# A capped-attention and swish feed-forward kernel: output sums kept in DRAM instead of SBUF

## The chip, the cores and the metric

The kernel runs on one core of a Trainium2 chip, as one program. The metric is the device time of one execution in microseconds (us); the number given for a kernel is the median of its timed runs. The traces come from one profiled execution each; their clock starts at the first instruction.

## What is computed

```python
scores = cap * tanh(q @ k.T / sqrt(64) / cap)       # 4 batches, 12 heads, 448 tokens
attn = exp(scores - max) / (sum + 1e-09)
x = heads side by side of (attn @ v)                # 1792 tokens x 768
h = x @ w_in                                        # 768 x 2048
out = (h * sigmoid(h)) @ w_out                      # 1792 tokens x 768, float32
```

The attention comes first and leaves x in SBUF; the feed-forward part (called moe in the code) follows on the same core.

## The kernel before, in words

The weights arrive as 64-bit floats and are turned into 32-bit ones on the core (`decode`, whose steps alternate between ACT and DVE). To keep precision, each operand of the moe's matmuls is split into a high part and a small remainder, and every product is made of three matmuls: high by high, remainder by high, high by remainder.

The moe works through 16 slices of 128 hidden features (NF = 16), taken two at a time: 8 passes, `fp` = 0 to 7. The 1792 tokens are cut into four blocks, three of 512 tokens and one of 256. Two kinds of unit fill a pass:

- `h_unit` (L585): 18 matmuls that make the hidden values of one slice for one block in a PSUM bank. `gate` (L603) follows it: ACT's sigmoid, DVE's product, ACT's copy of the high part and, one slot later, DVE's subtraction for the remainder. Eight such units make a pass.
- `o_unit` (L629): 12 matmuls that multiply 128 gated tokens by the two slices' rows of w_out. The result, 128 tokens by 768, lies in one of three PSUM tiles `s`, in two halves of 384 columns (NO2). `add` (L655) takes it out of PSUM. Fourteen such units make a pass, one for each group of 128 tokens.

The order is written out by hand in `moe` (L673): o_units come in pairs, and one or two h_units lie between pairs. Inside a slot, what belongs to earlier slots is issued first (L711 to L717), then the slot's own gate or add. Each engine works through its own queue strictly in the order of issue. Under `manual_schedule` (L726) this order is kept as it is written.

In `add`, the sums of all passes live in SBUF: 14 tiles `acc` of 128 x 768, six in one pool and eight in a second pool, `acc2`, which is opened at L422 when the attention's last buffers are free. For each half, DVE copies the PSUM tile into `acc` in the first pass (L665) and adds it in the other seven (L667). In the last pass SyncE's queue (SP) stores the finished rows to `out` (L671): one transfer of 384 KB for each unit, and for the very last unit, named LAST, two of 192 KB, one for each half. LAST also makes its halves one after the other (L637), the second in a PSUM bank of its own.

GpSimd (POOL) issues loads of q, k, v and the first weights during the attention (L295, L299, L292, L552 to L556); after that it issues nothing. SP issues the remaining weight loads of the moe (L552 to L556).

At the end stands a fallback (L733 to L735). Every engine loads a flag (TENSOR_LOAD, L733) and branches on it (COMPARE_BRANCH, L734) past a general version of the kernel, `tile_general`, which does not run here. A hint for that branch is set for SP and DVE alone (L724). Behind the branch come each engine's closing waits and drains; the trace puts these on line 794, where the kernel's outermost block ends.

Of the kernel before, what the change touches and what calls it, by code (L numbers as in the profile page):

```python
# [9 lines left out]
F32 = mybir.dt.float32  # L10
# [3 lines left out]
AF = mybir.ActivationFunctionType  # L14
ALU = mybir.AluOpType
# [170 lines left out]
def tile_softcap_attention_swish_moe(  # L186
# [12 lines left out]
    nc = tc.nc  # L199
# [4 lines left out]
    NT, DM = out.shape  # L204
# [7 lines left out]
    NO2 = DM // 2  # L212
# [6 lines left out]
    core = ctx.enter_context(ExitStack())  # L219
# [13 lines left out]
    pool = lambda st, name, bufs, **kw: st.enter_context(tc.tile_pool(name=name, bufs=bufs, reuse_waits="tile", **kw))  # L233
# [106 lines left out]
    def flat(t):  # L340
        return t.rearrange("p a s -> p (a s)")
# [67 lines left out]
    def norm2(s, parts=(0, 1)):  # L409
        b, u = s // NU, s % NU  # L410
        cs = slice(b * S, (b + 1) * S)
        x = U[s]
        if 0 in parts:
            nc.vector.tensor_tensor(flat(x), flat(x), flat(RB.pop(s)), ALU.mult)
        if 1 not in parts:
            return
        xh, xl = XH[:, 2 * u:2 * u + 2, cs], XL[:, 2 * u:2 * u + 2, cs]
        nc.vector.tensor_copy(xh, x)
        nc.vector.tensor_tensor(xl, x, xh.bitcast(F32), ALU.subtract)
        if s == NS - 1:  # L420
            tail.close()
            MPOOL["acc2"] = pool(core, "acc2", 1, side="right")  # L422


    BACK = {
# [19 lines left out]
    def attention():  # L445
# [17 lines left out]
        for s in range(NS):  # L463
# [33 lines left out]
            if s + 1 == NS:  # L497
                norm2(s - 2)
# [8 lines left out]
            for t in (i, k):  # L507
                for n in range(2):
                    exp(t, n)
                    sums(t, n)  # L510
                if 1 < s < NS - 1:
                    norm2(s - 2, (t - i,))
                for j in range(KC):
                    pv(t, j)
# [4 lines left out]
        pv_rem(s)  # L519
        u_vals(s)  # L520
        norm2(s - 1)
        pv_sum(s)
        u_sums(s)
# [13 lines left out]
    NFP = NF // G  # L537
    NTT = NT // 128
    MPOOL = {}
# [109 lines left out]
                        )  # L649
        return pa  # L650

    ACC = {}
    LAST = (NFP - 1, NB - 1, (NT - blocks[-1][0]) // 128 - 1)

    def add(fp, blk, t, pa):  # L655
        tt = blocks[blk][0] // 128 + t
        if tt not in ACC:
            ACC[tt] = MPOOL["acc" if tt < 6 else "acc2"].tile([128, DM], F32, name=f"acc{tt}")
        a = ACC[tt]
        last = (fp, blk, t) == LAST  # L660
        for e in range(2):
            c0, c1 = e * NO2, (e + 1) * NO2
            ae = a[:, c0:c1]
            if fp == 0:
                nc.vector.tensor_copy(ae, pa[e][:, 0:NO2])  # L665
            else:
                nc.vector.tensor_tensor(ae, pa[e][:, 0:NO2], ae, ALU.add)  # L667
            if fp == NFP - 1 and (last or e == 1):
                c0 = c0 if last else 0
                row = slice(128 * tt, 128 * tt + 128)  # L670
                nc.sync.dma_start(out=out[row, c0:c1], in_=a[:, c0:c1])  # L671

    def moe():  # L673

# [31 lines left out]
        for n, (bg, c) in enumerate(seq):  # L706
            if c[0] == "h":
                ps = h_unit(*c[1:])
            else:
                ps = o_unit(*c[1:])  # L710
            back(n, 0)  # L711
            late = list(LATE)
            LATE.clear()
            for x in late:
                gate(*x)
            for m, steps in bg:
                decode(m, steps)  # L717
            if c[0] == "h":
                gate(*c[1:], ps)
            else:  # L720
                add(*c[1:], ps)
            back(n, 1)
            if n == len(seq) - 3:
                tc.mark_branch_hint_location("short", 0, engines=[mybir.EngineType.SP, mybir.EngineType.DVE])  # L724
# [74 lines left out]
```

## Time and profile before

| what | value |
|---|---|
| median of 3 timed runs | 632.49 us |
| lowest and highest of them | 632.38 and 633.51 us |
| span of the profiled execution | 629.8 us |
| TensorE (PE) busy in the span | 621.0 us, 99% |
| DVE busy | 423.7 us, 67% |
| ACT busy | 271.0 us, 43% |
| POOL busy | 39.7 us, 6% |
| granted TensorE clock, mean | 1.000 |

The span runs from the first to the last instruction that the profile shows. For the profiled execution the span is the only time there is; the timed median lies 2.7 us above it (632.49 - 629.8), which is what an execution has around its instructions. PE, DVE, ACT and POOL are engines, PEld is TensorE's weight load, SP is SyncE. A letter q behind an engine's name (POOLq, SPq) marks instructions of its sequencer, such as waits, branches and DMA issues, which don't count as busy time. Where a row says "to landing", it gives the time from the issue of a DMA until its data and its semaphore had arrived.

### The profile page before, as it was taken

The numbers are of one execution on the slowest core, as the hardware profiler recorded it, in microseconds if no ns is written. First come the engines' busy times: TensorE is split into PE (matmuls) and PEld (weight loads), VectorE is DVE, ScalarE is ACT, GpSimd is POOL, SyncE is SP. The second block draws the span as 40 slices with busy tenths as digits, with TensorE's granted clock in tenths as the row PEclk, the third lists the DMA queues.
The fourth block names the chain that finished last, engine by engine and source line by source line (L and its number), as shares of the span: only waits on it lengthen the run. The fifth ranks groups of instructions, "written<-read, shape, count | busy, mean of one in ns | idle before, by whom it ended". The sixth has DMA issues, their size and how long they took to land.

```text
span 629.8 us, 9243 instructions
## 1 busy us (share of the span) xinstructions
PE 621.0 (99%) x3750; PEld 483.8 (77%) x3750; DVE 423.7 (67%) x661; ACT 271.0 (43%) x333; POOL 39.7 (6%) x75
## 2 busy tenths in 40 slices
PE   7999999999999999999999999999999999999996
PEld 3333333334699989999998999899989989999996
DVE  1578889889775685755684677558656856674343
ACT  7999999999213222322322322222223323222110
POOL 2231331320000000000000000000000000000000
PEclk9999999999999999999999999999999999999999
DMA  6674766461220421212130222212121302100224
GB/s 198 181 223 133 224 184 170 134 223 43 48 51 1 150 52 51 50 51 51 50 101 1 60 67 75 50 51 52 50 52 51 100 1 51 50 1 2 100 101 154
DMA packets 21507, 54.16 MB, mean 86 GB/s; under 512 B 4753, under 2 KB 13457, under 8 KB 21457
## 3 DMA queue, kind: packets, MB, share of 16 engines
q1 hardware_dynamic: 16928, 33.53, 19.5%
q0 software_dynamic: 4528, 19.96, 10.1%
q8 instruction: 31, 0.51, 0.3%
q14 instruction: 20, 0.16, 0.1%
HBM read 42.47 MB, written 5.51 MB: 76 GB/s over the span
## 4 chain that ended last, share of the span: by engine, by line
PE 97%; ACT 1%; DMA 1%; SPq 0%; issue 0%; DVE 0%
PE s L643 37%; PE h L592 36%; PE o L363 9%; PE s L308 8%; PE s L380 3%; PE o L370 1%; PE s L320 1%; DMA QK<-in_qkv_dram 1%; PE s L592 1%; ACT P L338 1%; ACT P L330 0%; PE h L643 0%; ACT P L334 0%; SPq L295 0%; DVE acc L667 0%
## 5 line engine op out<-in xcount | busy, mean ns | idle before, releaser
L592 PE MATMUL h<-XH,w 128*128 128x512 f32 (+1 forms) x756 | 217.5, 363 | 0.0
L643 PE MATMUL s<-w,gh 128*128 128x384 f32 x892 | 191.3, 335 | 0.0
L643 PEld LDWEIGHTS s<-w,gh 128*128 128x128 f32 x892 | 157.9, 188 | 2.9
L592 PEld LDWEIGHTS h<-XH,w 128*128 128x128 f32 x756 | 136.7, 188 | 22.1 <-DVE U L387 0.7
L592 PE MATMUL h<-XL,w 128*128 128x512 f32 (+1 forms) x378 | 137.5, 364 | 0.0
L607 ACT ACTIVATE gf<-h 128x512 f32<-128x512 f32 (+1 forms) x63 | 34.2, 543 | 206.3 <-PE h L592 205.9
L643 PE MATMUL s<-w,gl 128*128 128x384 f32 x446 | 113.7, 335 | 0.0
L608 DVE TENSOR_TENSOR gf<-h,gf 128x512 f32<-128x512 f32 (+1 forms) x63 | 39.3, 623 | 106.6 <-ACT gf L607 106.5
L667 DVE TENSOR_TENSOR acc<-s,acc 128x384 f32<-128x384 f32 x195 | 99.2, 550 | 8.6 <-PE s L643 8.5
L643 PEld LDWEIGHTS s<-w,gl 128*128 128x128 f32 x446 | 80.9, 188 | 0.0
L592 PEld LDWEIGHTS h<-XL,w 128*128 128x128 f32 x378 | 71.2, 188 | 10.4
L338 ACT ACTIVATE P<-P,capt 128x896 f32<-128x896 f32 (+1 forms) x60 | 75.0, 1328 | 0.0
L330 ACT ACTIVATE P<-s,sct 128x896 f32<-128x896 f32 x72 | 65.8, 1004 | 3.8 <-DVE over L265 3.6
L618 DVE TENSOR_TENSOR gl<-gf,gh 128x512 fp32r<-128x512 f32 (+1 forms) x64 | 40.1, 626 | 38.9 <-ACT gh L614 38.9
L614 ACT ACTIVATE gh<-gf 128x512 fp32r<-128x512 f32 (+1 forms) x64 | 37.1, 579 | 59.3 <-DVE gf L608 59.3
L308 PE MATMUL s<-QK 64*64 64x448 f32 x576 | 59.5, 542 | 1.0 <-DMA QK<-in_qkv_dram 1.0
L363 PE MATMUL o<-P,VT 128*64 128x448 f32 x288 | 58.1, 547 | 1.8 <-ACT P L338 1.7
L363 PEld LDWEIGHTS o<-P,VT 128*64 128x64 f32 x288 | 18.6, 136 | 40.5 <-issue 22.2
L308 PEld LDWEIGHTS s<-QK 64*64 64x64 f32 x576 | 20.7, 133 | 36.8 <-ACT P L330 15.7
L575 ACT ACTIVATE w<-RAW 128x768 fp32r<-128x768 f32 x28 | 23.7, 845 | 57.0 <-DVE RAW L180 50.4
L169 ACT ACTIVATE KRV<-RAW 128x768 f32<-128x768 f32 x28 | 25.0, 893 | 16.5 <-DVE RAW L180 11.6
L577 DVE TENSOR_TENSOR w<-RAW,w 128x768 fp32r<-128x768 f32 x32 | 30.5, 953 | 1.3 <-ACT w L575 1.2
(65 smaller groups left out, 366.8 us busy)
## 6 DMA issues: line engine op xcount, KB each, us to landing
QK<-in_qkv_dram POOLq DMA_DIRECT2D x21, 480.0 KB, 4.1
RAW<-in_moe_w_out_dram SPq DMA_DIRECT2D x13, 768.0 KB, 4.4
R<-RT SPq DMA_DIRECT2D x96, 56.0 KB, 2.7
RAW<-in_moe_w_in_dram SPq DMA_DIRECT2D x13, 384.0 KB, 4.2
RAW<-in_moe_w_in_dram SPq DMA_DIRECT2D x26, 192.0 KB, 4.7
out_dram<-acc SPq DMA_DIRECT2D x13, 384.0 KB, 2.3
VT<-in_qkv_dram POOLq DMA_DIRECT2D x22, 192.0 KB, 5.1
RAW<-in_moe_w_out_dram POOLq DMA_DIRECT2D x3, 768.0 KB, 8.1
```

What stands on the lines that cost most here:

```text
L308: nc.tensor.matmul(ps[half(c), e, 0:S], q[half(e), k0:k0 + 64], q[half(e), 0:S], start=True, stop=True)
L330: nc.scalar.activation(out=p, in_=SP.pop((i, j))[:, :, 0:S], func=AF.Tanh, scale=sct[:, 0:1])
L338: nc.scalar.activation(out=p, in_=p, func=AF.Exp, scale=capt[:, 0:1])
L363: nc.tensor.matmul(O[s][half(e), e ^ t, 0:S], v, p, start=(j == 0), stop=False)
L577: nc.vector.tensor_tensor(WS[m][:, 1], f, WS[m][:, 0].bitcast(F32), ALU.subtract)
L592: nc.tensor.matmul(ps[:, 0:n], w[:, a, kk * 128:(kk + 1) * 128], x[:, kk, t0:t0 + n], start=(kk == 0 and a == 0 and x is XH), stop=(kk == ...
L607: nc.scalar.activation(out=gf[:, 0:n], in_=ps[:, 0:n], func=AF.Sigmoid)
L608: nc.vector.tensor_tensor(gf[:, 0:n], ps[:, 0:n], gf[:, 0:n], ALU.mult)
L614: nc.scalar.activation(out=gh[:, 0:n], in_=gf[:, 0:n], func=AF.Copy)
L618: nc.vector.tensor_tensor(gl[:, 0:n], gf[:, 0:n], gh[:, 0:n].bitcast(F32), ALU.subtract)
L643: nc.tensor.matmul(pa[e][:, 0:NO2], g[a][:, ts], w[:, b, e * NO2:(e + 1) * NO2], start=(z == 0 and a == 0 and b == 0), stop=(z == G - 1 an ...
L667: nc.vector.tensor_tensor(ae, pa[e][:, 0:NO2], ae, ALU.add)
```

## The change

The sums move from SBUF to DRAM. `add` no longer keeps a tile for each group of tokens; each unit is copied out of PSUM into one of four rotating staging tiles `st`, the first half by ACT and the second by DVE. Then GpSimd's queue sends the staging tile to the output's rows: as a plain store in the first pass, and as an accumulating DMA, which adds to what lies there, in the seven others. Each unit sends one transfer of 384 KB; LAST sends two of 192 KB. SP no longer stores anything. The second pool `acc2` goes.

```diff
-            MPOOL["acc2"] = pool(core, "acc2", 1, side="right")
...
-    ACC = {}
...
         tt = blocks[blk][0] // 128 + t
-        if tt not in ACC:
-            ACC[tt] = MPOOL["acc" if tt < 6 else "acc2"].tile([128, DM], F32, name=f"acc{tt}")
-        a = ACC[tt]
+        a = MPOOL["acc"].tile([128, DM], F32, tag="st", name="st", bufs=4)
         last = (fp, blk, t) == LAST
+        row = slice(128 * tt, 128 * tt + 128)
         for e in range(2):
             c0, c1 = e * NO2, (e + 1) * NO2
-            ae = a[:, c0:c1]
-            if fp == 0:
-                nc.vector.tensor_copy(ae, pa[e][:, 0:NO2])
+            if e == 0:
+                nc.scalar.activation(out=a[:, c0:c1], in_=pa[e][:, 0:NO2], func=AF.Copy)
             else:
-                nc.vector.tensor_tensor(ae, pa[e][:, 0:NO2], ae, ALU.add)
-            if fp == NFP - 1 and (last or e == 1):
+                nc.vector.tensor_copy(a[:, c0:c1], pa[e][:, 0:NO2])
+            if last or e == 1:
                 c0 = c0 if last else 0
-                row = slice(128 * tt, 128 * tt + 128)
-                nc.sync.dma_start(out=out[row, c0:c1], in_=a[:, c0:c1])
+                if fp == 0:
+                    nc.gpsimd.dma_start(out=out[row, c0:c1], in_=a[:, c0:c1])
+                else:
+                    nc.gpsimd.dma_start(out=out[row, c0:c1], in_=a[:, c0:c1], accum_op=ALU.add)
```

## Rows read from the trace of the kernel before

**Rows 1.** The page, part 1: busy us (share of the span) and instructions.
```profile
span 629.8 us, 9243 instructions
PE 621.0 (99%) x3750; PEld 483.8 (77%) x3750; DVE 423.7 (67%) x661; ACT 271.0 (43%) x333; POOL 39.7 (6%) x75
```

**Rows 2.** Busy time by windows: attention, passes 2 and 7, and the end.
```profile
core 0: us, PE busy (x) PEld busy (x) DVE busy (x) ACT busy (x) POOL busy (x), PEclk, DMA share, GB/s
0.00:163.15 163.15, 159.10 (x1273) 56.80 (x1273) 126.73 (x159) 154.15 (x150) 39.66 (x75) 1.00 0.57 167
...
221.53:279.77 58.24, 58.24 (x313) 53.82 (x313) 42.08 (x71) 16.96 (x26) 0.00 (x0) 1.00 0.21 55
...
512.73:570.97 58.24, 58.24 (x313) 53.82 (x313) 37.91 (x64) 15.59 (x24) 0.00 (x0) 1.00 0.10 28
570.97:629.80 58.83, 54.09 (x294) 50.10 (x293) 24.57 (x45) 7.76 (x14) 0.00 (x0) 1.00 0.25 95
```

**Rows 3.** The chain that ended last, 400 to 460 us: start, us, what.
```profile
416.94 4.12 PE h L592 x18
421.06 4.18 PE s L643 x24
...
433.56 2.15 PE h L592 x18
435.70 4.16 PE s L643 x24
439.87 2.15 PE h L592 x18
442.02 4.16 PE s L643 x24
```

**Rows 4.** Groups by line and shape, 163.15 us to the end: busy us, mean ns.
```profile
L667 DVE TENSOR_TENSOR acc<-s,acc 128x384 f32<-128x384 f32 x195 | 99.2, 550 | 8.6 <-PE s L643 8.5
...
L607 ACT ACTIVATE gf<-h 128x512 f32<-128x512 f32 x47 | 28.1, 597 | 159.0 <-PE h L592 158.6
...
L665 DVE COPY acc<-s 128x384 f32<-128x384 f32 x28 | 14.1, 550 | 0.2 <-PE s L643 0.2
...
L607 ACT ACTIVATE gf<-h 128x256 f32<-128x256 f32 x16 | 6.1, 383 | 47.3 <-PE h L592 47.3
```

**Rows 5.** Timeline of DVE near the end: start us, us, instructions.
```profile
606.82 1.02 DVE L667 TENSOR_TENSOR acc<-s,acc 128x384 f32<-128x384 f32 x2
...
618.86 1.02 DVE L667 TENSOR_TENSOR acc<-s,acc 128x384 f32<-128x384 f32 x2 [0.27 <-PE s L643]
...
625.10 0.56 DVE L667 TENSOR_TENSOR acc<-h,acc 128x384 f32<-128x384 f32 x1 [0.49 <-PE h L643]
```

**Rows 6.** All DMA issues, GpSimd's queue: count, KB each, median us to landing.
```profile
QK<-in_qkv_dram POOLq DMA_DIRECT2D x21, 480.0 KB, 4.1
...
VT<-in_qkv_dram POOLq DMA_DIRECT2D x22, 192.0 KB, 5.1
RAW<-in_moe_w_out_dram POOLq DMA_DIRECT2D x3, 768.0 KB, 8.1
RAW<-in_moe_w_in_dram POOLq DMA_DIRECT2D x3, 384.0 KB, 7.2
RAW<-in_moe_w_in_dram POOLq DMA_DIRECT2D x6, 192.0 KB, 7.7
...
VB<-in_vrem_dram POOLq DMA_DIRECT2D x12, 48.0 KB, 4.9
```

**Rows 7.** By source line, L671 from 621 us: ns min/median/max, starts; landing us.
```profile
L671 SPq DMA_DIRECT2D out_dram<-acc x4: 332/348/912, 622.0 to 625.7; - x4
...
DMA to landing us min/median/max: 2.3/2.8/2.9
```

**Rows 8.** By source line, L295: GpSimd's QK issues, ns min/median/max, first and last start.
```profile
L295 POOL DMA_DIRECT2D QK<-in_qkv_dram x21: 536/553/795, 11.3 to 137.7; - x21
```

**Rows 9.** By source line, L299 from 137 us: GpSimd's last two issues, same columns.
```profile
L299 POOL DMA_DIRECT2D VT<-in_qkv_dram x2: 536/536/536, 138.2 to 138.8; - x2
...
DMA to landing us min/median/max: 3.9/3.9/4.0
```

**Rows 10.** By source line, L734: the branch past the fallback, same columns.
```profile
L734 POOLq COMPARE_BRANCH  x1: 45/45/45, 139.1 to 139.1; - x1
L734 POOLq EVENT_SEMAPHORE  x1: 17/17/17, 142.8 to 142.8; - x1
```

**Rows 11.** By source line, L794: GpSimd's closing instructions, near 143 and behind 629 us.
```profile
L794 POOLq DRAIN  x1: 5541/5541/5541, 142.9 to 142.9; - x1
...
L794 POOLq EVENT_SEMAPHORE  x4: 17/17/17, 629.0 to 629.7; - x4
L794 POOLq DRAIN  x2: 44/76/107, 629.2 to 629.5; - x2
```

## The prediction

> **What bounds the kernel now.** I read the busy times first: PE works 99% of the span [rows 1]. An average can hide a stage, so the stages come next. In passes 2 and 7 of the moe PE is busy for 58.24 us of 58.24 us at a granted clock of 1.00, while DVE works 38 to 42 us of a pass, ACT 16 to 17, POOL nothing, and the DMA engines are 10 to 21% busy [rows 2]. The chain of waits confirms it: unit follows unit with nothing between, a pair of o_units 4.18 us, an h_unit 4.12 or 2.15 us [rows 3]. So work that the change takes from DVE frees nobody that PE waits for: inside the passes there is no gain to be had, only stalls to be made. What is left is the end: behind PE's last matmul stand DVE's last addition, until 625.66 (625.10 + 0.56) [rows 5], SP's last store, issued at 625.7 and landed 2.3 us later [rows 7], and the closing waits until 629.8 [rows 1].
>
> **The copies.** 224 DVE instructions of 550 ns (28 copies and 196 additions) become 112 DVE copies and 112 ACT copies; a DVE copy of this shape costs the same 550 ns as an addition [rows 4]. DVE loses 14 x 0.55 = 7.7 us a pass. ACT's copy of 384 columns is not in the trace; between its 383 ns for 256 columns and 597 ns for 512 [rows 4] I take 490 ns, 6.9 us a pass, on an engine that has over 41 us of a pass free [rows 2]. Both hide under PE. ACT now waits for o_units in its queue, and behind such a wait stand the next slot's weight decoding and the next sigmoid. That sigmoid waits for an h_unit which ends 2.15 us or more after the pair [rows 3], so half a microsecond of copying is done by then: 0. The cost would go to 0.5 us for a slot, if a stall came between. In the last unit ACT's half is ready before DVE's, which ends at 625.66 as before.
>
> **The transfers inside the passes.** 113 transfers leave GpSimd's queue (111 whole units and two halves). Its issues take 536 to 795 ns [rows 8], 14 x 0.55 = 7.7 us of a pass in which POOL is idle: 0. SP loses 15 stores, and nothing behind them on SP is late: 0. A staging tile comes back after four units. The nearest such distance inside a pass is 606.82 to 618.86 = 12.0 us [rows 5]. Copy 0.55, issue 0.55 and the landing must fit: the landing may take 10.9 us. Landings of GpSimd's transfers are 4.1 to 8.1 us in the median [rows 6], so the buffers are back in time. A late one first costs the copy, not PE: three PSUM tiles stand between.
>
> The row that speaks of issue, 536 to 795 ns beside a DVE that was busy for 126.73 of 163.15 us [rows 2, 8], shows little waiting of POOL for DVE. The Trainium skill's page "SBUF — State Buffer", section "SBUF: two separate sides", says that a DMA issued from GpSimd starves while DVE runs certain copies, since both want one port, and the section behind it tells of 620 ns becoming 3100 ns. With 3.1 us an issue (an estimate from that page), 14 issues would take 43 us of a pass's 58, and the tile would still be back inside 12.0 us at a 5.1 us landing. So the sum stays at 0 by the rule as by the row.
>
> **DMA engines.** A pass sends 14 x 393,216 bytes = 5.5 MB, 95 GB/s, beside 55 GB/s of loads. The last stage, with its stores, moves 95 GB/s at a busy share of 0.25 [rows 2]. Plain stores would bring 0.21 + 0.25 = 0.46; if an accumulating transfer occupies an engine twice as long as a plain one, since the old sum must be read as well, 0.71. Both are below 1. No row has an accumulating DMA; it binds at about 3.2 times a plain store's time (0.79 / 0.25).
>
> **The end.** This is where I expect the time to change. GpSimd is now the last to issue. Before, it left early and unseen: its last issue began at 138.8 [rows 9], it branched at 139.1, its next instruction came at 142.8 [rows 10], and its drain began at 142.9 and took 5.54 us [rows 11]. That is 4.1 us from the last issue to the drain. It hid under 480 us of matmuls. The branch hint is for SP and DVE, not for POOL. Now the chain is: DVE's copy ends 625.66; issue at 625.7; drain may begin at 625.7 + 4.1 = 629.8. The last transfer lands later still: 192 KB by GpSimd's queue took 5.1 us in the median [rows 6], so 630.8. The bounds for it are 2.3 us, SP's store of that size [rows 7], and 8.1 us, the slowest kind of GpSimd's load [rows 6]. The drain of before also began just behind the last landing (138.8 + 3.9 = 142.7 [rows 9]), so its 5.54 us may count from there; I count it from the later one, 630.8 + 5.5 = 636.3. Behind it come the barrier and the clearing of semaphores, 629.0 to 629.8 = 0.8 us [rows 1, 11]. Sum: 637.1 against 629.8, so 7.3 us more.
>
> What the drain costs is the open price. Its bounds are 0.1 us, as GpSimd's other closing drains of 44 and 107 ns [rows 11], and a price for each DMA issued so far: 67 issues (21 + 22 + 3 + 3 + 6 + 12 [rows 6]) make 83 ns each, and 180 issues (67 + 113) would make 14.9 us. I take 5.5 us, because the only drain behind a row of transfers showed it. Nothing in the sum is negative: no row shows an instruction of the end that goes away without another in its place, except SP's store issue (332 ns at the shortest [rows 7]), which GpSimd's own issue replaces.
>
> The sum is made against the profiled span, 629.8 us. Added to the median of the runs, 632.49 + 7.3 = 639.8 us.
>
> **Rivals.**
>
> *A: the drain is short, and the landing ends the run.* For it: the drains at 629 us cost about 0.1 us [rows 11]. Against: the one at 142.9 us had no transfer left to wait for and still took 5.54 us. Landing at 630.8, then SP's waits as long as before (from the last landing at 628.0 to the barrier at 629.0 [rows 7, 11]), then 0.8: 632.6, 2.8 us more, 635.3 us; with landings of 3.9 to 8.1 us, 634.1 to 638.3.
>
> *C: the drain grows with the issues.* For it: 5.54 us is long for a single flush, and 67 transfers stood before it. Against: nothing shows that all are kept until the end. At most 630.8 + 14.9 + 0.8 = 646.5, 16.7 us more: 649.2 us.
>
> *D: the stream stalls.* Either the accumulating transfers fill the DMA engines, or each waits for the one before because all write the same tensor. For it: no row has such a transfer. Against: SP's last stores go out within less than the 2.8 us that one takes to land (four between 622.0 and 625.7, one of them held by its data) [rows 7], so rows of the output don't wait for each other. At four times a plain store the share is 1.21, and seven passes grow by 0.21 x 58.24 = 12.2 us each: 718 us. In strict series a pass takes 14 x (0.55 + 5.1) = 79 us: 21 us more in each of eight passes, some 800 us.
>
> *N: not slower.* The one mechanism is GpSimd's way out: if its drain costs 0.1 us and the accumulating transfer lands within about 3.3 us of its issue, at 629.0, the run ends near 629.8 + 0.1 + 0.8 = 630.7 even with the branch as slow as before, 0.9 us later: 633.4 us, no change that can be told. It decides from a landing below 3.3 us; SP's stores reach 2.3 [rows 7], GpSimd's quietest load 3.9 [rows 9].
>
> A gain would need PE to have waited for DVE's additions, and the full passes deny it [rows 2].
>
> **How the numbers follow.** Forecast 0.42; A 0.20; C 0.20; D 0.10; N 0.06; a gain from something that no row shows, 0.02. A measurement of this kernel can tell about 0.2%, 1.3 us. Forecast, A, C and D lie above that: slower 0.92, same 0.06, faster 0.02. The range goes from A with an early landing, 634.0, to C near its upper end, 648.5; D, N and the gain, 0.18, lie outside. The forecast's own range is 638.8 (landing no later than 629.8) to 642.8 (landing after 8.1 us).
>
> **What would show it.** Right: passes of 58.24 us with PE full; ACT copies of about 0.49 us; GpSimd issues of 0.5 to 0.8 us; PE's last matmul still at 625; POOL's branch some 3.7 us from its next instruction, then a POOL drain of 5 us or more with all other engines waiting, and an end near 637.1. A drain near 0.1 us makes it A or N, one near 15 us makes it C. Passes longer than 58.5 us, with PE waiting for PSUM tiles behind ACT, would make it D and prove the sum wrong where it holds the transfers at 0.

## The result, and the profile after

The changed kernel takes 640.19 us in the median (639.9 to 640.33, 4 runs), the kernel before 632.88 us (632.38 to 633.51, 4 runs). The ratio is 1.0114, with a 95% interval of 1.0102 to 1.0127: 7.3 us slower. The forecast was 639.8 us, between 634.0 and 648.5.

The stages stand as forecast. First the page's busy times and the windows of pass 2, pass 7 and the end of the changed kernel; the columns are those of [rows 1, 2].

```profile
span 638.4 us, 9632 instructions
PE 621.5 (97%) x3750; PEld 483.9 (76%) x3750; DVE 373.5 (59%) x549; ACT 322.4 (51%) x445; POOL 132.2 (21%) x188
```

```profile
221.53:279.77 58.24, 58.24 (x313) 53.82 (x313) 36.27 (x57) 23.46 (x42) 11.89 (x15) 1.00 0.75 162
...
512.73:570.97 58.24, 58.24 (x313) 53.82 (x313) 31.67 (x52) 21.99 (x38) 12.00 (x14) 1.00 0.70 123
570.97:639.00 68.03, 55.48 (x302) 51.48 (x301) 17.96 (x32) 15.86 (x30) 14.54 (x17) 0.93 0.59 94
```

A pass still takes 58.24 us with PE busy for all of it, while DVE has lost some 6 us of a pass, ACT has gained 6 and GpSimd (POOL) 12, and the DMA engines have gone from 0.10 to 0.70 of their time in pass 7 [rows 2]. The last window alone is worse.

The groups by line and shape of the changed kernel, from 163 us on, show the new copies and transfers (busy us, mean ns | idle before).

```profile
L669 POOL DMA_DIRECT2D out_dram<-st x99 | 84.8, 862 | 314.7 <-DVE st L663 302.3 <-issue 7.8 <-DVE KRV L176 4.6
...
L663 DVE COPY st<-s 128x384 f32<-128x384 f32 x111 | 61.3, 553 | 44.2 <-ACT st L661 44.1
L661 ACT ACTIVATE st<-s 128x384 f32<-128x384 f32 x112 | 54.0, 489 | 72.3 <-PE s L642 65.4 <-ACT KRV L169 4.7
...
L667 POOL DMA_DIRECT2D out_dram<-st x14 | 7.6, 547 | 80.6 <-DVE st L663 80.6
```

ACT's copy takes 489 ns where [rows 4] had been read as 490. DVE waits for ACT's half (44.1 us in all); that both write the same staging tile is the likely reason. Nothing behind them is late. GpSimd needs 862 ns to issue an accumulating transfer (L669) against 547 ns for a plain one (L667).

Then the end, behind PE's last matmul. The last PE row of the timeline, first of the kernel before, then of the changed one (start us, us):

```profile
624.73 0.34 PE L643 MATMUL h<-w,gl 128*128 128x384 f32 x1
```

```profile
626.11 0.34 PE L642 MATMUL h<-w,gl 128*128 128x384 f32 x1
```

PE ends at 625.07 and 626.45 us. The 1.4 us between them arise in the first 11 us: PE's first group of L320 begins at 10.07 us before and at 11.39 us after, and from there to the end of its last matmul it takes 615.0 and 615.1 us. The first small load, `capt`, landed later in this execution (DVE waited 5.8 us for it instead of 4.2, by the view of waits), which is the likely reason. What counts is the distance from PE's last matmul to the end of the span: 629.81 - 625.07 = 4.7 us before, 638.38 - 626.45 = 11.9 us after. That is 7.2 us more, as much as the timed runs show. Here are the last transfers, the branch past the fallback, GpSimd's closing instructions and SP's, each by source line (ns min/median/max, first and last start us), to be held against [rows 7, 9 to 11].

```profile
out_dram<-st POOLq DMA_DIRECT2D x111, 384.0 KB, 5.5
...
out_dram<-st POOLq DMA_DIRECT2D x2, 192.0 KB, 7.1
```

```profile
L669 POOL DMA_DIRECT2D out_dram<-st x4: 847/977/1191, 623.7 to 627.3; - x4
...
DMA to landing us min/median/max: 5.7/6.5/7.3
```

```profile
L732 POOLq COMPARE_BRANCH  x1: 45/45/45, 628.3 to 628.3; - x1
L732 POOLq EVENT_SEMAPHORE  x1: 17/17/17, 628.8 to 628.8; - x1
```

```profile
L792 POOLq EVENT_SEMAPHORE  x4: 17/17/17, 637.6 to 638.3; - x4
L792 POOLq DRAIN  x3: 50/107/8647, 628.9 to 638.1; - x3
```

```profile
L792 SPq EVENT_SEMAPHORE  x14: 17/28/18426, 615.8 to 638.3; - x14
L792 SPq DRAIN  x3: 7/7/13, 635.0 to 637.8; - x3
```

The last transfer is issued at 627.3 and lands 6.9 us later, at 634.2; SP's wait that began at 615.8 and took 18.4 us ends with it. SP has finished its waits at 635.0. GpSimd's drain began at 628.9 and takes 8.65 us, until 637.55; all engines wait for it, and the span ends 0.8 us later. (The other engines' closing semaphores come at 637.7.) So the end was set by GpSimd's drain, as forecast, but by other pieces than forecast: a branch of 0.5 us in place of 3.7, a landing of 6.9 in place of 5.1, a drain of 8.65 in place of 5.5.

### The profile page after: what moved, and what is told of

Its sections match the earlier page's. It is cut to its first block, busy times and chain, and to the rows that moved or that the text cites. A ratio compares the mean times of both kernels' runs of the same rounds, so it can differ in the third digit from the quotient of the medians.

```text
span 638.4 us, 9632 instructions
## 1 busy us (share of the span) xinstructions
PE 621.5 (97%) x3750; PEld 483.9 (76%) x3750; DVE 373.5 (59%) x549; ACT 322.4 (51%) x445; POOL 132.2 (21%) x188
## 5 line engine op out<-in xcount | busy, mean ns | idle before, releaser
L669 POOL DMA_DIRECT2D out_dram<-st x99 | 84.8, 862 | 314.7 <-DVE st L663 302.3
L661 ACT ACTIVATE st<-s 128x384 f32<-128x384 f32 x112 | 54.0, 489 | 72.3 <-PE s L642 65.4
L663 DVE COPY st<-s 128x384 f32<-128x384 f32 x111 | 61.3, 553 | 44.2 <-ACT st L661 44.1
L591 PEld LDWEIGHTS h<-XL,w 128*128 128x128 f32 x378 | 71.2, 188 | 10.4
```

The lines of the kernel that those rows point to most:

```text
L591: nc.tensor.matmul(ps[:, 0:n], w[:, a, kk * 128:(kk + 1) * 128], x[:, kk, t0:t0 + n], start=(kk == 0 and a == 0 and x is XH), stop=(kk == ...
L661: nc.scalar.activation(out=a[:, c0:c1], in_=pa[e][:, 0:NO2], func=AF.Copy)
L663: nc.vector.tensor_copy(a[:, c0:c1], pa[e][:, 0:NO2])
L669: nc.gpsimd.dma_start(out=out[row, c0:c1], in_=a[:, c0:c1], accum_op=ALU.add)
```

## The experiments

Two theories of the drain were set against each other. W: it works through the transfers that GpSimd still holds, each for some 80 ns, whether landed or not; a drain earlier in the run would take that work off the end. L: it costs a fixed time behind the last landing. Beside them stood the forecast's D (the passes pay) and, from the second group of runs on, A (the accumulation pays, not the queue). PE's last matmul ends up to 1.6 us apart in the runs, all of it from the first 11 us as above (from L320's first group to that end, each of the twelve takes 615.0 to 615.2 us). So the table has the distance from PE's last matmul (start plus duration of the last PE row) to the end of the span. Each distance comes from one trace; e2, e4, e7, e8 and e9 were timed once. The three kernels that end with SP's stores differ by 0.2 us.

| run | PE's last matmul ends | span ends | distance | closing drain | GpSimd's issues |
|---|---|---|---|---|---|
| before | 625.07 | 629.81 | 4.7 | hidden | 67 |
| after | 626.45 | 638.38 | 11.9 | 8.65 | 180 |
| e1_drain | 625.91 | 635.38 | 9.5 | 6.40 | 180 |
| e2_plain | 626.41 | 636.03 | 9.6 | 6.60 | 180 |
| e3_sp_last | 625.84 | 630.77 | 4.9 | hidden | 165 |
| e4_only_last | 626.55 | 642.40 | 15.9 | 6.76 | 82 |
| e5_pool_store | 626.15 | 639.29 | 13.1 | 6.77 | 82 |
| e6_readback | 626.34 | 631.23 | 4.9 | hidden | 165 |
| e7_drain_one | 625.27 | 634.76 | 9.5 | 1.91 | 82 |
| e8_drain_plain | 626.63 | 632.71 | 6.1 | 2.89 | 180 |
| e9_hint | 625.90 | 635.67 | 9.8 | 6.77 | 82 |
| e10_hint_drain | 626.49 | 632.88 | 6.4 | 3.37 | 82 |

**e3_sp_last: do the passes pay?**

```diff
                 if fp == 0:
                     nc.gpsimd.dma_start(out=out[row, c0:c1], in_=a[:, c0:c1])
+                elif fp == NFP - 1:
+                    nc.sync.dma_start(out=out[row, c0:c1], in_=a[:, c0:c1])
                 else:
```

> The last pass's transfers go out by SP's queue as plain stores; passes 1 to 6 still accumulate by GpSimd's queue. The output lacks the addition of the last pass to the others. If the whole cost stands at the end (both W and L): GpSimd is done 35 us or more before the end, the stretch from PE's last matmul to the end falls from 11.9 us to the 4.7 us of the kernel before, time 632.9. If the passes cost something (theory D of the prediction): time above 633.5 and passes longer than 58.24 us.

632.81 us against 632.4 for the kernel before, ratio 1.0010 (1.0000 to 1.0019), and a distance of 4.9 us. With 165 of the 180 transfers still in place the cost is gone, but for 0.2% at most. It stands in the last pass's transfers, not in the passes: D falls. GpSimd's drain now lies far from the end, and after 165 issues it is short; in e6, with as many, it takes the same 3.74 us.

```profile
L794 POOLq DRAIN  x3: 50/107/3739, 578.9 to 630.5; - x3
```

**e6_readback: the same, with the whole result**

```diff
+        if fp == NFP - 1:
+            while len(BACKSUM) < min(NTT, tt + 4):
+                n = len(BACKSUM)
+                BACKSUM[n] = MPOOL["acc"].tile([128, DM], F32, tag="rd", name="rd", bufs=4)
+                nc.sync.dma_start(out=BACKSUM[n], in_=out[128 * n:128 * n + 128, :])
         for e in range(2):
             c0, c1 = e * NO2, (e + 1) * NO2
-            if e == 0:
+            if fp == NFP - 1:
+                nc.vector.tensor_tensor(a[:, c0:c1], pa[e][:, 0:NO2], BACKSUM[tt][:, c0:c1], ALU.add)
+            elif e == 0:
...
+                elif fp == NFP - 1:
+                    nc.sync.dma_start(out=out[row, c0:c1], in_=a[:, c0:c1])
```

> A mended version that computes all of it: passes 0 to 6 keep the sums in DRAM as in the changed kernel; in the last pass SP reads each group's sums back into SBUF, three groups ahead, DVE adds them to the PSUM tile, and SP stores the result. GpSimd issues nothing in the last 50 us. If the cost stands only at the end, the end is that of the kernel before, 4.7 us behind PE's last matmul: time 632.4 to 632.8. If the passes pay for the transfers: above 633.5.

632.83 us against 632.58, ratio 1.0002 (0.9993 to 1.0012): no difference that can be told. Its DMA issues show that the sums come back from DRAM in 4.1 us and the last stores land in 2.6:

```profile
out_dram<-st POOLq DMA_DIRECT2D x98, 384.0 KB, 5.8
...
rd<-out_dram SPq DMA_DIRECT2D x14, 384.0 KB, 4.1
out_dram<-st SPq DMA_DIRECT2D x13, 384.0 KB, 2.9
...
out_dram<-st SPq DMA_DIRECT2D x2, 192.0 KB, 2.6
```

Sums in DRAM cost no time, then, as long as the last pass ends without GpSimd.

**e1_drain: an earlier drain**

```diff
+                if (fp, blk, t) == (NFP - 1, 0, 0):
+                    nc.gpsimd.drain()
                 if fp == 0:
```

> One more drain of GpSimd is put ahead of the last pass's first transfer; all else is as in the changed kernel. Theory W (the drain works through the transfers issued since the last drain, some 83 ns each, up to a limit of about 105): the early drain lasts 5 us or more and hides under the passes; the closing one has 15 transfers to work through and so ends within 0.5 us of the last landing instead of 3.3 us behind it. The span falls by about 2.5 us to 635.9, the time to about 637.7. Theory L (the drain costs a fixed time behind the last landing, whatever the number): the closing drain still ends 3.3 us behind the landing, span 638.4, time 640.2. Both: passes of 58.24 us.

637.13 us, ratio 1.0077 (1.0060 to 1.0095) instead of 1.0114; the distance falls from 11.9 to 9.5 us. GpSimd's early drain, its closing one, and its last issues:

```profile
L667 POOLq DRAIN  x1: 7720/7720/7720, 573.3 to 573.3; - x1
```

```profile
L794 POOLq DRAIN  x1: 6402/6402/6402, 628.0 to 628.0; - x1
```

```profile
L671 POOL DMA_DIRECT2D out_dram<-st x4: 847/978/1191, 623.2 to 626.8; - x4
...
DMA to landing us min/median/max: 6.3/6.6/6.9
```

The early drain takes 7.7 us beside the matmuls, where nobody waits for it. The closing one ends at 634.40, 0.7 us behind the last landing (626.8 + 6.9 = 633.7), where the changed kernel's ended 3.3 us behind it (637.55 - 634.23). L falls: the time behind the landing depends on whether GpSimd's queue was cleared before.

**e2_plain: no accumulation**

```diff
-                if fp == 0:
-                    nc.gpsimd.dma_start(out=out[row, c0:c1], in_=a[:, c0:c1])
-                else:
-                    nc.gpsimd.dma_start(out=out[row, c0:c1], in_=a[:, c0:c1], accum_op=ALU.add)
+                nc.gpsimd.dma_start(out=out[row, c0:c1], in_=a[:, c0:c1])
```

> All transfers of GpSimd's queue are plain stores, as many and as large as before; the output then holds only the last pass's part, the additions over passes are left out. Both theories: packets of the stores take half as long for their bytes, landings near the 2.6 us of the first pass's plain stores instead of 5.8, the last one 3 to 4 us earlier. Theory W: the number of transfers is the same, so the closing drain still takes 8.7 us or more (up to 14.9 if more transfers are kept until the end) and the span stays at 638 us or grows, up to 644. Theory L: the drain ends 3.3 us behind a last landing near 630.5, span near 634.6.

Neither theory's number came: a span of 636.0, between W's 638 and L's 634.6. The last store landed 3.4 us behind its issue, yet the drain went on for 6.60 us, 4.5 us past that landing (4.5, not 3.3, so no fixed price). W's price for the drain, 8.7 us or more, missed too: after the same 180 issues it took 2 us less than in the changed kernel, so the number of issues alone doesn't set it. W can stand only if fewer than 180 transfers are held to the end.

```profile
L789 POOLq DRAIN  x3: 44/107/6602, 628.6 to 635.8; - x3
```

**e8_drain_plain: both taken away**

```diff
+                if (fp, blk, t) == (NFP - 1, 0, 0):
+                    nc.gpsimd.drain()
+                nc.gpsimd.dma_start(out=out[row, c0:c1], in_=a[:, c0:c1])
```

> Plain stores only (the additions over passes are left out of the output) and the extra drain ahead of the last pass. What is left at the end is GpSimd's queue alone: last landing about 4.3 us behind PE's last matmul, then 0.1 to 1.3 us of drain, then 0.8: the run ends 5.9 to 6.5 us behind PE's last matmul, against 4.7 before, 9.5 with accumulation and the extra drain, and 9.6 with plain stores and no extra drain. Theory L (a fixed price behind the landing): about 9.6, as without the extra drain.

6.1 us, as W says. GpSimd's closing drain and its last issues:

```profile
L791 POOLq DRAIN  x1: 2887/2887/2887, 628.9 to 628.9; - x1
```

```profile
L668 POOL DMA_DIRECT2D out_dram<-st x3: 539/542/542, 626.0 to 627.5; - x3
...
DMA to landing us min/median/max: 3.4/3.5/3.6
```

The drain begins at 628.9 and ends 2.89 us later, 0.7 us behind the last landing (627.5 + 3.6 = 631.1). What is left over SP's 4.7 us is 1.4 us: the plain store by GpSimd's queue lands later, 3.4 to 3.6 us behind its issue against SP's 2.3 [rows 7], and the drain adds its 0.7 us where SP's waits took 1.0. Pass 7 of this run, by windows, has the DMA engines' share with plain stores (the columns of [rows 2]):

```profile
512.73:570.97 58.24, 58.24 (x314) 53.82 (x313) 31.67 (x51) 21.98 (x39) 8.27 (x14) 1.00 0.36 123
```

The bytes are those of the changed kernel in that pass, 123 GB/s; the share is 0.36 where accumulation has 0.70.

**e4_only_last and e7_drain_one: the count**

```diff
-                if fp == 0:
-                    nc.gpsimd.dma_start(out=out[row, c0:c1], in_=a[:, c0:c1])
-                else:
+                if fp == NFP - 1:
+                    if (blk, t) == (0, 0):
+                        nc.gpsimd.drain()
                     nc.gpsimd.dma_start(out=out[row, c0:c1], in_=a[:, c0:c1], accum_op=ALU.add)
```

(The first of the two is without the drain and its condition.)

> The transfers of passes 0 to 6 are left out, the copies out of PSUM stay; the last pass's 15 transfers accumulate as in the changed kernel. The output lacks passes 0 to 6. GpSimd then issues 82 transfers in all instead of 180. Theory W: the closing drain takes 82 x 83 ns = 6.8 us instead of 8.65, or ends with the last landing if that is later; the stretch from PE's last matmul to the end falls from 11.9 to about 10 us. Theory L: the drain ends 3.3 us behind the last landing, 11.9 us.

The drain was as W says, the end was not: 82 transfers, 6.76 us, but a distance of 15.9 us instead of 10. GpSimd's branch took 6.2 us this time, so that the drain only began behind the landing:

```profile
L730 POOLq COMPARE_BRANCH  x1: 45/45/45, 628.5 to 628.5; - x1
L730 POOLq EVENT_SEMAPHORE  x1: 17/17/17, 634.7 to 634.7; - x1
```

```profile
L790 POOLq DRAIN  x3: 50/107/6761, 634.8 to 642.1; - x3
```

Here nothing was left to land, and the drain still took 6.76 us. With the kernel before, 67 transfers and 5.54 us [rows 11], that gives (6.761 - 5.541) / 15 = 81 ns for a transfer, and 67 x 81 = 5.4 us of the 5.54. The packets of GpSimd's queue are not what counts: 6688 here and 5696 in e5 below, with the same drain. Bytes, 19.96 and 25.47 MB, fit less well: 1.22 us / 5.51 MB x 19.96 MB makes 4.4 us of the 5.54.

> As the run with only the last pass's transfers (passes 0 to 6 left out of the output), with one more drain of GpSimd ahead of the first of them. Theory W: the early drain finds the attention's 67 transfers, all long landed, and takes 5.5 us, as the closing drain of the kernel before; the closing one has 15 to work through instead of 82 and takes about 1.3 us behind the last landing instead of 6.8. A fixed price of a drain would give the two drains the same length.

The closing drain was short, 1.91 us from 632.0, and ended 0.7 us behind the last landing. The early one took 6.66 us instead of 5.5. It began at 138.8, before GpSimd's last load of the attention was issued (139.0 + 0.54 = 139.5), so 0.7 of the 1.1 us lie ahead of the end of that issue. The same holds for the early drain of e10 below (6.82 us from 140.0, the last issue over at 140.7). The last loads were still under way as well (landed 3.7 us after their issue); the other 0.4 us stay open.

```profile
L299 POOL DMA_DIRECT2D VT<-in_qkv_dram x2: 538/538/538, 138.4 to 139.0; - x2
```

```profile
L668 POOLq DRAIN  x1: 6660/6660/6660, 138.8 to 138.8; - x1
```

```profile
L792 POOLq DRAIN  x1: 1914/1914/1914, 632.0 to 632.0; - x1
```

**e5_pool_store, e9_hint and e10_hint_drain: the queue without the change**

These three are the kernel before, with its sums in SBUF; e9 has e5's edit and the hint, e10 those and the drain.

```diff
+                if (blk, t) == (0, 0):
+                    nc.gpsimd.drain()
-                nc.sync.dma_start(out=out[row, c0:c1], in_=a[:, c0:c1])
+                nc.gpsimd.dma_start(out=out[row, c0:c1], in_=a[:, c0:c1])
...
-engines=[mybir.EngineType.SP, mybir.EngineType.DVE])
+engines=[mybir.EngineType.SP, mybir.EngineType.DVE, mybir.EngineType.Pool])
```

> The kernel before, with its sums in SBUF; only the last pass's 15 stores go out by GpSimd's queue instead of SP's, plain. It changes who issues last, and nothing else. Theory W (GpSimd's closing drain works through every transfer it still holds, 81 to 83 ns each): 67 + 15 = 82 transfers, 6.8 us of drain, which begins between the branch (about 2.2 us behind PE's last matmul, as in the runs with the fast branch) and the last landing (about 4.3 us behind it, as with plain stores): the run ends 9.8 to 12 us behind PE's last matmul instead of 4.7, time 637.5 to 639.7. Rival A (the accumulation is what costs, not the queue): only the later landing counts, 1.4 us, time near 633.8.

640.33 us against 632.58, ratio 1.0121 (1.0104 to 1.0139): a little above W's 639.7 and far from A's 633.8. Fifteen plain stores moved from SP's queue to GpSimd's cost as much as the whole change. Its branch and its drain:

```profile
L734 POOLq COMPARE_BRANCH  x1: 45/45/45, 627.7 to 627.7; - x1
...
L734 POOLq EVENT_SEMAPHORE  x1: 17/17/17, 631.6 to 631.6; - x1
```

```profile
L794 POOLq DRAIN  x3: 44/107/6766, 631.7 to 639.0; - x3
```

> The kernel with its sums in SBUF whose last 15 stores go by GpSimd's queue, with the branch hint set for GpSimd too. If the 3.9 us between GpSimd's branch and its next instruction there is code that has to be fetched: it falls to 0.4 to 0.5 us, as for the hinted engines, and the drain begins near 2.2 us behind PE's last matmul instead of 5.5. The drain still has 82 transfers to clear, 6.8 us, of which a part must wait for the landing 4.5 us behind PE: the run ends 10 to 12 us behind PE's last matmul instead of 13.1. If the branch waits for the transfers to land instead: nothing changes, 13.1 us.

9.8 us instead of 13.1. The branch takes 0.5 us; the drain begins 3.6 us earlier, while transfers are still under way, and takes the same 6.77 us:

```profile
L734 POOLq COMPARE_BRANCH  x1: 70/70/70, 627.5 to 627.5; - x1
L734 POOLq EVENT_SEMAPHORE  x1: 17/17/17, 628.0 to 628.0; - x1
```

```profile
L794 POOLq DRAIN  x3: 40/109/6772, 628.1 to 635.4; - x3
```

So the slow branch was a missing hint here and not a wait for the transfers, and the drain's work runs beside their landing: after 82 issues it takes 6.76 to 6.77 us in all three runs (e4, e5, e9), begun before the landing or after it. The rule in the Trainium skill's page "Runtime: NRT & Kernel Launch", section "Instruction fetch mechanics", that a taken branch whose target isn't at hand must fetch it first, agrees with 3.9 us without the hint and 0.5 us with it.

> The same with one more drain of GpSimd ahead of the last pass's first store, so that 15 transfers are left for the closing drain instead of 82. If the transfers still held set the drain's length, the closing drain ends within 0.7 us of the last landing, the run ends about 6.1 us behind PE's last matmul (4.5 for the landing, 0.7, 0.9), against 4.7 for SP's stores: time about 634.0. If a fixed price stands behind the landing, 10 us or more, time 638 or above.

634.68 us against 632.64, ratio 1.0031 (1.0018 to 1.0044), a distance of 6.4 us (0.3 us over the expectation): the drain ends 632.04, 0.7 us behind a landing at 631.4. Of the 7.8 us that GpSimd's queue had cost in e5 (640.33 - 632.58), the two edits take back 5.7 (640.33 - 634.68).

```profile
L796 POOLq DRAIN  x1: 3373/3373/3373, 628.7 to 628.7; - x1
```

No run points to a version faster than the kernel before: PE fills the passes, and the 4.7 us behind it are shorter than any end through GpSimd that was run.

## Why the prediction was right

**Right and shown.** The passes give and cost nothing: 58.24 us before and after, and e3 and e6 keep 165 transfers at no cost. ACT's copies took 489 ns for 490, and no copy waited for a staging tile, though the margin was thin: the longest landing of an accumulating transfer was 10.4 us, where the prediction had room for 10.9. The loss stands behind PE's last matmul, because GpSimd is now last to leave, and its drain sets the end: e1 moves 2.4 us of it away, e3 and e6 all but 0.2 us, e5 makes it without the rest of the change.

Two sizes inside the passes were missed and cost nothing there. DVE lost 5.8 to 6.2 us of a pass instead of 7.7, mainly because the two additions of a unit had taken 1.02 us together [rows 5] and not twice 0.55. An accumulating issue took 0.86 us instead of 0.5 to 0.8, so GpSimd works 12.0 us of a pass instead of 7.7.

**Right in the sum, wrong in its terms.** From PE's last matmul the forecast had 637.1 - 625.07 = 12.0 us, and 11.9 were measured. That the two agree within 0.1 us is luck: along the path the last issue came 0.85 us behind PE instead of 0.63 (+0.2), the landing took 1.8 us more, and what the drain adds behind the landing was 2.2 us less.

- Branch: "4.1 us from the last issue to the drain". Measured 1.6 us (627.3 to 628.9). It is no part of the cancelling, as the landing came later than the branch in the forecast as in the run. GpSimd's branch needs 0.5 us without a hint in the four kernels with 180 issues (after, e1, e2, e8) and 3.7 to 6.2 us in the six others without one (before, e3 to e7). The forecast took one observation for a property of the kernel.
- Landing: "192 KB by GpSimd's queue took 5.1 us in the median". Measured 6.9. e8's plain stores land within 3.6 us at the same place, so 3.3 of them are the accumulation. The share of the DMA engines shows its price: the stores raise pass 7 from 0.10 [rows 2] to 0.70, and e8's plain stores only to 0.36, so an accumulating transfer takes (0.70 - 0.10) / (0.36 - 0.10) = 2.3 times a plain one. The forecast had put in 2 for the share and nothing for the landing. The last two pairs of units follow each other without an h_unit, 2.09 us a unit, and the transfers queue up: from 625 to 629 us the DMA engines' share is 1.08, which is full, and still 0.91 in the 4 us behind, where e8 has 0.71 from 625 to 629 us.
- Drain: "I count it from the later one", 5.5 us behind the landing. Measured 3.3 us behind it and 8.65 in all. By e9 its work begins before the landing, and between 67 and 82 issues it grows by 81 ns for each. That is rival C's mechanism, though not its size: 180 issues would have made 14.6 us. With 165 issued, the hidden drains of e3 and e6 took 3.74 us, so some seem to be cleared on the way; which ones, and when, no run shows.

The 7.2 us can be divided: 11.9 to 9.5 by clearing GpSimd's queue earlier (e1), 2.4 us; 9.5 to 6.1 by leaving out the accumulation as well (e8), 3.4 us; what is left, 6.1 to 4.7, goes with GpSimd in place of SP, 1.4 us. The first two shares depend on the order: leaving out the accumulation first (e2) takes 2.3 us, and the earlier drain then 3.5, presumably because landing and clearing run side by side. The last step is not one edit; e8 and the kernel before differ in the whole change but the accumulation.

The page "Collectives: The Full Stack", section "The bandwidth ceiling: the fold count and why AG ≠ RS ≠ AR", of the Trainium skill says of the reducing step of a ring collective that its add needs two source reads, so that it runs at half the rate of the copying step. The 2.3 above lies near that, for another kind of transfer; no run here shows that the second read is the reason.

The starving of GpSimd's issues by DVE, which the prediction weighed by the page "SBUF — State Buffer" of the Trainium skill, was not seen in the issues: the longest of 99 took 1.19 us, none 3.1.

**Open.** How many transfers GpSimd held when the changed kernel's drain began, and so which part of its 8.65 us was waiting and which was clearing. Why early drains that begin with transfers under way are longer after 165 issues (7.72 us in e1 and 5.95 in e8, against 3.74 begun after the landing in e3 and e6): the last issue, still running, makes at most 0.9 us of it, as it makes more than half of the difference after 67 (e7, e10). Why GpSimd's branch is fast in the changed kernel without a hint; that its target then lies in code already fetched was not tried.

## What to carry to other kernels

Moving a kernel's last stores to GpSimd's queue puts GpSimd's own way out, branch and drain, at the end of the run, though the profile of before shows both as harmless in the middle: look up what an engine does behind its last instruction before making it the last. If GpSimd must finish, drain it once while the matmuls still cover it and hint its branch (e5 to e10: 13.1 to 6.4 us); better, let SP's stores end the kernel (4.7 to 4.9 us). An accumulating DMA beside a full PE can be free in all passes but the last, as here, and still be dear for the last few units, where its landing has no cover.

## What the runs showed of the hardware

- GpSimd's drain is not a fixed price: 5.54 us with 67 transfers issued and 6.76 to 6.77 with 82, also where all of them had landed, but 3.74 with 165 (e3, e6). With an earlier drain it ended about 0.7 us behind the last landing, in four runs (e1, e7, e8, e10).
- An accumulating transfer of 384 KB costs GpSimd 0.86 us to issue against 0.55 for a plain one, and 2.3 times the time on the DMA engines.
- GpSimd's branch past the same fallback took 0.5 us in four kernels and 3.7 to 6.2 us in six others; with a hint 0.5 us (e9, e10).
